# An attention kernel that splits its exponentials between two engines: three weighted pieces instead of four equal ones on VectorE

## The chip, the cores and the metric

The kernel runs on one core of one Trainium2 chip. The metric is the device time of one execution in microseconds (us). Most executions agree within 0.3%. Five engines matter: PE (TensorE, matrix multiply), DVE (VectorE), ACT (ScalarE), POOL (GpSimd) and SP (SyncE, which issues transfers). They run their own fixed lists of instructions and wait for each other by semaphores.

## The reference, cut to what matters

Two attention branches share the input x (2048 x 512, 32 heads of 16 columns). Branch A is full softmax attention, branch B a local one over 8 earlier positions with stride 2. A sigmoid gate mixes them.

```python
q, k, v = qkv[0], qkv[1], qkv[2]                      # 32 heads, 2048 positions, 16 columns
scores = jnp.einsum("bhqd,bhkd->bhqk", q, k) * scale   # 32 x 2048 x 2048 values
p = _softmax(scores, axis=-1)
o = jnp.einsum("bhqk,bhkd->bhqd", p, v)
...                                                    # branch B: 8 positions per query
return g * a + (1 - g) * b
```

Branch A asks for 32 x 2048 x 2048 exponentials. The kernel cuts them into 2048 items of 128 keys x 512 queries (128 partitions x 512 columns).

## The kernel before

ACT computes the exponential of two or three items at a time (1024 or 1536 columns), straight from the score banks, the memory into which PE writes the scores. DVE takes the other items by an arithmetic form: it writes a scaled and shifted score as a 16-bit integer, whose bits, read as a 16-bit float, are a rough exponential ("first piece"). Copies of it with another integer added are the same curve, shifted ("second-stage pieces"), made for up to four items at once. PE multiplies each piece with the values v and adds all pieces up, so that their errors partly cancel. Before, there are four pieces with equal weight:

```python
PW_S = tuple(s - math.log2(4.604879) for s in (0.0, 0.51171875, 0.1953125, -0.22070312))
NP_ = len(PW_S)
...
def exp_dve(slot_item):            # first piece: 512 columns, from a score bank
    return nc.vector.tensor_scalar(out=self.yb[bt["buf"]][:, 0, i * 512:(i + 1) * 512], in0=bank[:],
                                   scalar1=A, scalar2=1024.0 * (15.0 + PW_S[0]), op0=ALU.mult, op1=ALU.add)
def piece(bt, k):                  # second-stage piece k: up to 4 items at once
    return nc.vector.tensor_scalar(out=y[:, k, 0:n], in0=y[:, 0, 0:n],
                            scalar1=float(round(1024.0 * (PW_S[k] - PW_S[0]))), scalar2=None, op0=ALU.add)
...
nc.scalar.activation(out=self.pt[pi[0]][pi[1]][:, 0:n * 512],      # ACT: 2 or 3 items
                     in_=self.aslot[si][:, 0:n, :].rearrange("p a b -> p (a b)"), func=ACT.Exp, scale=SCALE)
...
nc.tensor.matmul(out=out, lhsT=v, rhs=r, start=start, stop=stop, tile_position=(0, 32 * j))  # weighted values
```

The order of all instructions is fixed when the program is built: the kernel's own scheduler walks through the work with its estimates of durations and decides, group by group, whether DVE takes items. "The plan of limits" is a table of 64 settings for each of eleven rules (how much work may wait for DVE, when PE turns to other work, and so on), one setting for each 32 items. A key tile is 128 keys, a key chunk four key tiles; the keys are made ready chunk by chunk, and DVE copies each result from its bank (its "evacuation"). A group of scores is held back until the keys that it may need are ready:

```python
def kq_ok(self, rem, geo, p, n, now):
    ...
        kts = sorted(kt for r in rem[b] for kt in r)[:n - left]
        ...
        for d in [self.qdone.get((ct, qc))] + [self.kdone.get((ct, kt // 4)) for kt in kts if ct or kt]:
            if d is not None and (d.end is None or d.end > now):
                return False
```

The lines of the profile name these places: L1509 (first piece), L1515 (second-stage pieces), L1580 (weighted values), L1774 (scores) and L1828 (ACT's exponentials). In the changed kernel the same five are L1533, L1539, L1605, L1801 and L1855.

Of the kernel before, what the change touches and what calls it, by code (L numbers as in the profile page):

```python
# [19 lines left out]
P = 128  # L20
S = 2048
D = 512
H = 32
# [13 lines left out]
SAFE_A = 8.5  # L37
BDEN_MIN, BDEN_MAX = 1e-30, 1e30

PW_S = tuple(s - math.log2(4.604879) for s in (0.0, 0.51171875, 0.1953125, -0.22070312))  # L40
NP_ = len(PW_S)

ACT_W = (3, 2)
NPT = (4, 4)
# [18 lines left out]
    order=((-1, 1, 0, 2, 3), (-1, 0, 2, 1, 3), (-1, 0, 1, 2, 3), (-1, 0, 1, 2, 1), (1, 0, 1, 2, 3)),  # L63
)
STRETCH = dict(
    backlog="2123224322422022220413433124322022122202222223242202222242220222",
    backlog_s="2222222312432222422021322322222202212222042122213222222022222323",
    part_us="2220421041243222243202020241242042210223124202210222222222222220",
    misc_slack="0004233313424222221242320140242224122321112121323222222242210222",
    urgent="2322222222200222222212213221131222034112012232322222222021222222",  # L70
    fit="2241222322244222322212212022422212422422222223222222222222222222",
    port="2220222202243220222020324222224422222202222222221322222222301322",
    alone="2212222122222114022222243221222222222322242231222232222233002222",
    grab="1222212222214222222222222222222224421342244213222222222422222422",
    lend="2220222222231202222224132222224232322212222244232122222242212422",
    order="2222432212022222320131412123232222203202222020223222222222222222",
)
SLOT_D = 3
D_LAST = 58
# [6 lines left out]
def _ap(t, offset, dims):  # L86
    return bass.AP(t.tensor, offset, [list(d) for d in dims])

def head_of(g, j):
    return 8 * (g // 2) + (g % 2) + 2 * j  # L90
# [654 lines left out]
class _Fast:  # L745
# [15 lines left out]
    def setup(self):  # L761
# [9 lines left out]
        self.qs = [c([P, 512], BF16, name=f"qs{i}") for i in range(2)]  # L771
        self.vaug = c([P, NKT * H * VS + 32], BF16, name="vaug")
        self.vaug4 = self.vaug[:, 0:NKT * H * VS].rearrange("p (t h e) -> p t h e", t=NKT, h=H, e=VS)
        self.pt = [[c([P, w * 512], BF16, name=f"pt{a}_{i}") for i in range(n)]
                   for a, (w, n) in enumerate(zip(ACT_W, NPT))]
        self.yb = [c([P, NP_, YB_ITEMS * 512], I16, name=f"yb{i}") for i in range(NYB)]
# [66 lines left out]
        nc.gpsimd.memset(self.vaug4[:, :, :, DH:VS], 1.0)  # L843
        nc.gpsimd.memset(self.vaug4[:, :, 8, 0:DH], 0.0)
        nc.gpsimd.memset(self.vaug[:, NKT * H * VS:NKT * H * VS + 32], 0.0)
        nc.gpsimd.memset(self.halo[:], 0.0)
        self.idx = pidx, pf, ei, ef
        nc.gpsimd.memset(self.ones[:], 1.0)
# [48 lines left out]
    def v_evac(self, st0, nst, h0, h1):  # L897
        n = (h1 - h0) * DH
        self.nc.vector.tensor_copy(out=self.vaug4[:, st0:st0 + nst, h0:h1, 0:DH],  # L899
                                   in_=self.misc[:, 0:nst * n].rearrange("p (t h e) -> p t h e", t=nst, e=DH))  # L900

    def k_evac(self, ct, sc):
        self.nc.vector.tensor_copy(out=self.kT[ct % 2][:, sc * 512:(sc + 1) * 512], in_=self.misc[:])
# [93 lines left out]
    def jobs(self):  # L997
# [58 lines left out]
                                               n=16 if (ct, sc) == (3, 3) else 8)  # L1056
        for st in range(0, NKT, 2):
            ch = self.chain([("PE", 2 * 4 * 0.06, lambda st=st: self.v_mm(st, 2, 0, 8)),
                             ("DVE", T_D1(256), lambda st=st: self.v_evac(st, 2, 0, 8))],
                            due=4 * st - 4 if st else -20, rel=max(1, 4 * st), deps=xs[st // 4])  # L1060
            vdone[(0, st)] = vdone[(0, st + 1)] = ch[-1]
        for st in range(NKT):
            ch = self.chain([("PE", 4 * 0.162, lambda st=st: self.v_mm(st, 1, 8, H)),
                             ("DVE", T_D1(384), lambda st=st: self.v_evac(st, 1, 8, H))],
                            due=512 - 100 + 4 * st, rel=80 + 20 * st)
            for ct in range(1, 4):
                vdone[(ct, st)] = ch[-1]
# [368 lines left out]
    def run(self):  # L1436
# [81 lines left out]
        def close_batch():  # L1518
            nonlocal batch
            bt = batch  # L1520
            batch = None
            n = len(bt["items"]) * 512
            bt["refs"] = NP_ * len(bt["items"])
            parts = [dict(n=NP_) for _ in bt["items"]]

            def done(k, end):
                for i, it in enumerate(bt["items"]):
                    add_pv(it, self.yb[bt["buf"]][:, k, i * 512:(i + 1) * 512].bitcast(F16), end, ("y", bt), parts[i])
            for k in range(1, NP_):
                s = Step("DVE", T_D4(n), lambda k=k: piece(bt, k), deps=list(bt["p1"]), due=bt["due"], cls=2)  # L1530
                s.on_done = lambda end, k=k: done(k, end)
                s.port = True
                self.steps.append(s)  # L1533
            last = bt["p1"][-1]

            def after(end, prev=last.on_done):
                prev(end)
                done(0, end)
            if last.end is None:  # L1539
                last.on_done = after  # L1540
            else:
                done(0, last.end)
# [9 lines left out]
        def emit_pv_one(j, now):  # L1552
            b, kt, r, ready, src, part = pvq[j].pop(pv_first(j, now))
            if b not in acc:
                acc_take(b)
            ct, qc, par = geo(b)
            g = 2 * ct + par
            first = (b, j) not in started
            started.add((b, j))
            part["n"] -= 1  # L1560
            if part["n"] == 0:
                jleft[(b, j)] -= 1
                left[b] -= 1
            last = jleft[(b, j)] == 0
            kind, ref = src
            if kind == "p":
                pt_refs[ref] -= 1
                if pt_refs[ref] == 0:
                    pt_free[ref] = now + 0.45
            else:  # L1570
                ref["refs"] -= 1
                if ref["refs"] == 0:
                    yb_free[ref["buf"]] = now + 0.45
            out = self.flex[acc[b]][32 * j:32 * j + 32, :]
            parts = [(g, r, out)] if b < NB - 2 else [(2 * ct + k, r[:, 256 * k:256 * k + 256], out[:, 256 * k:256 * k + 256])
                                                      for k in range(2)]

            def mm(g, r, out, start, stop):
                v = _ap(self.vaug, self.vaug4[:, kt, head_of(g, j), 0:1].offset, [self.vaug.ap[0], [1, 32]])
                nc.tensor.matmul(out=out, lhsT=v, rhs=r, start=start, stop=stop, tile_position=(0, 32 * j))  # L1580
            return [lambda k=k, a=a: mm(*a, first and k == 0, last and k == len(parts) - 1) for k, a in enumerate(parts)]

# [115 lines left out]

        def d_wanted(now, flex=True):

            if p >= N - 8 or p % 64 >= D_LAST:
                return False
            if batch is None and min(yb_free) > now:
                return False
            if flex and min(fx_free) > now:
                return False
            ready = [s for s in self.steps if s.rel <= p and s.eng in ("PE", "DVE") and ready_time(s) <= now + 1.5]
            if flex and any(s.acq and s.due <= p + tune("misc_slack") for s in ready):
                return False
            load = max(0.0, t["DVE"] - now) + sum(s.cost for s in ready if s.eng == "DVE")  # L1710
            return load < tune("backlog" if flex else "backlog_s")

        def draw(used, dve=False):


            nonlocal p
            b = p // 64
            js = [j for j in range(4) if rem[b][j]]
            js = [j for j in js if j not in used] or js
            if dve:  # L1720
                bj = [it[2] for it in batch["items"]] if batch is not None else []
                j = min(js, key=lambda j: (j in bj, dcount.get((b, j), 0), -len(rem[b][j]), j))
            else:
                j = min(js, key=lambda j: (-len(rem[b][j]), j))
            used.append(j)
            p += 1
            return b, rem[b][j].pop(0), j

        def d_add(it, bank, p1done):
            nonlocal batch  # L1730
# [58 lines left out]
        while True:  # L1789
# [173 lines left out]
                            wake = min(wake, est)  # L1963
            if not did:
                t[eng] = max(min(wake, max(others, now) + 0.02 if others > now else now + 0.02), now + 0.005)
        self.BP["2"].release()

    def kq_ok(self, rem, geo, p, n, now):
        left = 0
        for b in range(p // 64, NG * NQC):  # L1970
            ct, qc, par = geo(b)
            kts = sorted(kt for r in rem[b] for kt in r)[:n - left]
            left += len(kts)
            for d in [self.qdone.get((ct, qc))] + [self.kdone.get((ct, kt // 4)) for kt in kts if ct or kt]:
                if d is not None and (d.end is None or d.end > now):
                    return False
            if left >= n:
                break
        return True
# [31 lines left out]
```

## Time and profile before

The kernel before took 744.03 us (median of 3 runs, 743.74 to 744.54). Its page of the profiled execution says, in the part on busy time and the part on 40 slices of the span (each digit is the busy share of one slice in tenths):

```profile
span 741.4 us, 21444 instructions
PE 705.9 (95%) x8713; PEld 233.9 (32%) x8713; DVE 692.8 (93%) x1180; ACT 723.2 (98%) x699; POOL 204.4 (28%) x212
...
ACT  6999999999999999999999999999999999999994
```

ACT is busy except in the first and the last slice. The stretches view (busy us of each engine in a window, with the number of instructions) shows how complete this is in the middle:

```profile
80.00:120.00 40.00, 39.28 (x486) 12.23 (x483) 39.52 (x68) 39.96 (x40) 0.00 (x0) 1.00 0.10 22
400.00:440.00 40.00, 37.78 (x403) 11.65 (x399) 37.88 (x64) 40.00 (x37) 22.70 (x20) 1.00 0.46 124
```

The columns are the length, then PE, PE's weight loads, DVE, ACT and POOL, then the clock and the transfers. ACT stands at 39.96 and 40.00 of 40 us. PE and DVE are close to full too. The Trainium skill ("Perfetto Trace Analysis", Identifying the Most-Contended Engine) says that occupancy is a fair measure for ACT and DVE, and a poor one for matmuls.

ACT's timeline (start, duration of the record, instruction) gives the cost of one exponential:

```profile
299.12 1.19 ACT L1828 ACTIVATE pt_2_85<-fps 128x1024 bf16<-128x1024 f32 x1
300.03 1.20 ACT L1828 ACTIVATE pt_0_87<-fps 128x1024 bf16<-128x1024 f32 x1
300.93 1.64 ACT L1828 ACTIVATE pt_1_84<-fps 128x1536 bf16<-128x1536 f32 x1
302.26 1.23 ACT L1828 ACTIVATE pt_1_88<-fps 128x1024 bf16<-128x1024 f32 x1
```

The records overlap: they last 1.19 and 1.64 us, but the starts are 0.91 and 1.33 us apart. Only the distance of starts may be summed. With 484 exponentials of 1024 columns at 0.9065 us and 201 of 1536 at 1.333 us, ACT's list is 706.7 us long and holds 1571 of the 2048 items.

DVE's part, in the view of groups kept apart by shape (count, busy us, mean ns of one record, idle time before and its releaser), one of three buffers shown of each:

```profile
L1509 DVE TENSOR_SCALAR yb_92<-fps 128x512 int16<-128x512 f32 x162 | 106.2, 679 | 6.7 <-PE fps L1774 6.3
L1515 DVE TENSOR_SCALAR yb_92<-yb_92 128x2048 int16<-128x2048 int16 x111 | 73.0, 686 | 0.3
```

A second-stage piece of four items costs as much as a first piece of one item (both about 0.60 us start to start): it reads 16-bit data from SBUF, the first piece reads a score bank. This fits the Trainium skill ("VectorE: DVE Perf Modes", Mode 4×_2P), which gives four elements per cycle for such operands.

The head, that is the first 40 us, in which inputs are still being prepared, from ACT's timeline:

```profile
8.22 1.02 ACT L1828 ACTIVATE pt_0_83<-fps 128x1024 bf16<-128x1024 f32 x1 [0.54 <-PE fps L1774]
9.14 1.02 ACT L1828 ACTIVATE pt_0_87<-fps 128x1024 bf16<-128x1024 f32 x1
10.38 1.02 ACT L1828 ACTIVATE pt_1_84<-fps 128x1024 bf16<-128x1024 f32 x1 [0.22 <-PE fps L1774]
11.30 1.02 ACT L1828 ACTIVATE pt_1_88<-fps 128x1024 bf16<-128x1024 f32 x1
12.20 1.03 ACT L1828 ACTIVATE pt_2_85<-fps 128x1024 bf16<-128x1024 f32 x1
14.88 1.02 ACT L1828 ACTIVATE pt_2_89<-fps 128x1024 bf16<-128x1024 f32 x1 [1.65 <-PE fps L1774]
```

ACT starts at 8.22 us, does five exponentials (ten items), and then waits 1.65 us for scores.

### The profile page before, as it was taken

The numbers are of one execution on the slowest core, as the hardware profiler recorded it, in microseconds if no ns is written. First come the engines' busy times: TensorE is split into PE (matmuls) and PEld (weight loads), VectorE is DVE, ScalarE is ACT, GpSimd is POOL, SyncE is SP. The second block draws the span as 40 slices with busy tenths as digits, with TensorE's granted clock in tenths as the row PEclk, the third lists the DMA queues.
The fourth block names the chain that finished last, engine by engine and source line by source line (L and its number), as shares of the span: only waits on it lengthen the run. The fifth ranks groups of instructions, "written<-read, shape, count | busy, mean of one in ns | idle before, by whom it ended". The sixth has DMA issues, their size and how long they took to land.

```text
span 741.4 us, 21444 instructions
## 1 busy us (share of the span) xinstructions
PE 705.9 (95%) x8713; PEld 233.9 (32%) x8713; DVE 692.8 (93%) x1180; ACT 723.2 (98%) x699; POOL 204.4 (28%) x212
## 2 busy tenths in 40 slices
PE   9999999999999999998989999999999999999996
PEld 4422333333333222332222232332233232333343
DVE  6899999998999999999999999999899999899985
ACT  6999999999999999999999999999999999999994
POOL 2142000000003321322002555646544564534000
PEclk9999999999999999999999999999999999999999
DMA  5001010001000000001032546566555456422001
GB/s 165 3 18 50 8 39 1 2 2 46 2 9 9 23 1 3 8 2 38 23 118 84 147 130 160 129 137 152 140 142 128 105 125 156 120 72 58 9 23 35
DMA packets 63723, 48.59 MB, mean 66 GB/s; under 512 B 21760, under 2 KB 63232, under 8 KB 63488
## 3 DMA queue, kind: packets, MB, share of 16 engines
q1 hardware_dynamic: 62912, 45.70, 24.4%
q8 instruction: 70, 1.15, 0.7%
q0 software_dynamic: 288, 1.05, 0.4%
q10 hardware_dynamic: 416, 0.39, 0.2%
q14 instruction: 37, 0.30, 0.1%
HBM read 39.85 MB, written 5.26 MB: 61 GB/s over the span
## 4 chain that ended last, share of the span: by engine, by line
ACT 39%; PE 37%; issue 11%; DVE 10%; SPq 1%; DMA 0%; POOL 0%; ACTq 0%; DVEq 0%; POOLq 0%
PE fps L1774 13%; PE fps L1580 12%; PE fps L871 9%; ACT pt_0_83 L1828 6%; ACT pt_3_86 L1828 5%; ACT pt_2_85 L1828 5%; ACT pt_0_87 L1828 5%; ACT pt_3_90 L1828 5%; ACT pt_1_84 L1828 4%; ACT pt_2_89 L1828 4%; ACT pt_1_88 L1828 4%; DVE yb_92 L1509 2%; DVE yb_93 L1509 1%; DVE yb_91 L1509 1%; DVE yb_93 L1515 1%
## 5 line engine op out<-in xcount | busy, mean ns | idle before, releaser
L1580 PEld LDWEIGHTS <-vaug 128*32 128x32 bf16 x3697 | 86.3, 94 | 135.4 <-issue 112.2
L1828 ACT ACTIVATE pt_0_83<-fps 128x1536 bf16<-128x1536 f32 (+1 forms) x87 | 122.2, 1405 | 0.5 <-PE fps L1774 0.5
L1828 ACT ACTIVATE pt_3_86<-fps 128x1536 bf16<-128x1536 f32 (+1 forms) x85 | 117.5, 1382 | 0.0
L1828 ACT ACTIVATE pt_1_84<-fps 128x1536 bf16<-128x1536 f32 (+1 forms) x85 | 115.6, 1360 | 0.4 <-PE fps L1774 0.4
L1828 ACT ACTIVATE pt_2_85<-fps 128x1024 bf16<-128x1024 f32 (+1 forms) x86 | 115.4, 1341 | 0.1
L1509 DVE TENSOR_SCALAR yb_92<-fps 128x512 int16<-128x512 f32 x162 | 106.2, 679 | 6.7 <-PE fps L1774 6.3
L1509 DVE TENSOR_SCALAR yb_93<-fps 128x512 int16<-128x512 f32 x159 | 104.9, 680 | 5.4 <-PE fps L1774 5.1
L1509 DVE TENSOR_SCALAR yb_91<-fps 128x512 int16<-128x512 f32 x156 | 102.8, 679 | 7.7 <-PE fps L1774 7.4
L1580 PE MATMUL fps<-yb_92,vaug 128*32 128x512 f16 (+1 forms) x696 | 100.9, 368 | 0.0
L1580 PE MATMUL fps<-yb_93,vaug 128*32 128x512 f16 (+1 forms) x668 | 99.0, 373 | 0.7 <-DVE vaug L899 0.5
L1580 PE MATMUL fps<-yb_91,vaug 128*32 128x512 f16 (+1 forms) x664 | 98.8, 370 | 0.3 <-DVE yb_91 L1515 0.3
L871 PE MATMUL fps<-xT,ww 128*32 128x512 bf16 (+2 forms) x1296 | 98.1, 380 | 0.0
L1828 ACT ACTIVATE pt_2_89<-fps 128x1024 bf16<-128x1024 f32 x85 | 96.2, 1132 | 1.7 <-PE fps L1774 1.7
L1828 ACT ACTIVATE pt_0_87<-fps 128x1024 bf16<-128x1024 f32 x87 | 97.5, 1121 | 0.0
L1828 ACT ACTIVATE pt_3_90<-fps 128x1024 bf16<-128x1024 f32 x85 | 95.8, 1127 | 0.2 <-ACT pt_2_85 L1828 0.2
L1828 ACT ACTIVATE pt_1_88<-fps 128x1024 bf16<-128x1024 f32 x85 | 95.1, 1118 | 0.7 <-PE fps L1774 0.6
L1774 PEld LDWEIGHTS <-kT_73 32*128 32x128 bf16 x1024 | 47.2, 91 | 147.1 <-issue 144.1
L1774 PEld LDWEIGHTS <-kT_72 32*128 32x128 bf16 x1024 | 45.2, 91 | 145.0 <-issue 139.9
L1515 DVE TENSOR_SCALAR yb_92<-yb_92 128x2048 int16<-128x2048 int16 (+2 forms) x129 | 80.5, 655 | 0.4
L1515 DVE TENSOR_SCALAR yb_93<-yb_93 128x2048 int16<-128x2048 int16 (+3 forms) x126 | 79.5, 661 | 0.3
L1515 DVE TENSOR_SCALAR yb_91<-yb_91 128x2048 int16<-128x2048 int16 (+3 forms) x129 | 78.9, 642 | 0.2
L1177 POOL TENSOR_TENSOR prod_821<-bq_809,bk_810 128x512 bf16<-128x512 bf16 x32 | 34.0, 1076 | 114.7 <-DVE yb_93 L1515 52.6
(189 smaller groups left out, 1260.3 us busy)
## 6 DMA issues: line engine op xcount, KB each, us to landing
vw_5734<-v_dram SPq DMA_DIRECT2D x64, 128.0 KB, 3.1
vw_5735<-v_dram SPq DMA_DIRECT2D x64, 128.0 KB, 3.2
er<-er_dram SPq DMA_DIRECT2D x128, 64.0 KB, 3.1
erb_5730<-er_dram SPq DMA_DIRECT2D x64, 64.0 KB, 3.2
erb_5731<-er_dram SPq DMA_DIRECT2D x64, 64.0 KB, 3.3
out_dram<-ob SPq DMA_DIRECT2D x15, 128.0 KB, 1.8
ww<-in_B_wqkv_dram SPq DMA_DIRECT2D x12, 128.0 KB, 2.7
ww<-in_A_wqkv_dram SPq DMA_DIRECT2D x8, 128.0 KB, 3.1
```

Source lines behind the costliest of these rows:

```text
L871: self.nc.tensor.matmul(out=out_ps[32 * c:32 * c + 32, 0:n], lhsT=lhsT_of(c), rhs=rhs, start=start, stop=stop, tile_position=(0, 32 * c))
L1177: return e.tensor_tensor(out=pr[m % 2][:, a:b], in0=bq[ct][:, a:b], in1=bk[ct][:, o + a:o + b], op=ALU.mult)
L1509: return nc.vector.tensor_scalar(out=self.yb[bt["buf"]][:, 0, i * 512:(i + 1) * 512], in0=bank[:], scalar1=A, scalar2=1024.0 * (15.0 + PW_ ...
L1515: return nc.vector.tensor_scalar(out=y[:, k, 0:n], in0=y[:, 0, 0:n], scalar1=float(round(1024.0 * (PW_S[k] - PW_S[0]))), scalar2=None, op0 ...
L1580: nc.tensor.matmul(out=out, lhsT=v, rhs=r, start=start, stop=stop, tile_position=(0, 32 * j))
L1774: nc.tensor.matmul(out=dst, lhsT=self.kT[ct % 2][32 * j:32 * j + 32, kt * 128:(kt + 1) * 128], rhs=self.qm[(4 * ct + qc) % NQM][par][32 * ...
L1828: nc.scalar.activation(out=self.pt[pi[0]][pi[1]][:, 0:n * 512], in_=self.aslot[si][:, 0:n, :].rearrange("p a b -> p (a b)"), func=ACT.Exp, ...
```

## The change: its intent, and the diff

Three pieces with the weights 1, 1.265625 and 0.796875 take the place of four equal ones. This removes one second-stage instruction per batch from DVE and one weighted-value matmul per item of DVE from PE. The weights cannot sit in the pieces, so they sit in two scaled copies of v, kept for six of the sixteen key tiles only; DVE therefore takes items of these six key tiles, ACT prefers the others. DVE makes the copies, with 24 more instructions. The plan of limits was made anew.

```diff
-PW_S = tuple(s - math.log2(4.604879) for s in (0.0, 0.51171875, 0.1953125, -0.22070312))
+PW_W = (1.0, 1.265625, 0.796875)
+PW_S = tuple(s - math.log2(3.127444) for s in (0.0, -0.3330078125, 0.3330078125))
 NP_ = len(PW_S)
+KD = (2, 4, 7, 9, 12, 14)
...                                     # STRETCH: some settings of the plan changed
+    def v_scaled(self, st0, nst, h0, h1, k):
+        for st in range(st0, st0 + nst):
+            if st in KD:
+                self.nc.vector.tensor_scalar(out=self.vw4[k][:, KD.index(st), h0:h1, 0:DH], in0=...,
+                                             scalar1=PW_W[k], scalar2=None, op0=ALU.mult)
...
-                v = _ap(self.vaug, self.vaug4[:, kt, head_of(g, j), 0:1].offset, [self.vaug.ap[0], [1, 32]])
+                t_, t4, i = (self.vw[w], self.vw4[w], KD.index(kt)) if w else (self.vaug, self.vaug4, kt)
+                v = _ap(t_, t4[:, i, head_of(g, j), 0:1].offset, [t_.ap[0], [1, 32]])
...                                     # draw(): DVE's items come from KD, ACT's from the rest first
-            return b, rem[b][j].pop(0), j
+            kt = next((k for k in rem[b][j] if (k in KD) == dve), rem[b][j][0])
...                                     # kq_ok(): which keys a group of scores may need
-            kts = sorted(kt for r in rem[b] for kt in r)[:n - left]
+            kts = sorted(kt for r in rem[b] for kt in r if kt not in KD)[:n - left]
+            kts += sorted(kt for r in rem[b] for kt in r if kt in KD)[:n - len(kts) if len(kts) < n - left else 4]
```

More of the change, by code (lines that the diff above doesn't have):

```diff
@@ L38 @@
 BDEN_MIN, BDEN_MAX = 1e-30, 1e30
-PW_S = tuple(s - math.log2(4.604879) for s in (0.0, 0.51171875, 0.1953125, -0.22070312))
+PW_W = (1.0, 1.265625, 0.796875)
+PW_S = tuple(s - math.log2(3.127444) for s in (0.0, -0.3330078125, 0.3330078125))
 NP_ = len(PW_S)
+KD = (2, 4, 7, 9, 12, 14)
+NOT_KD = tuple(k for k in range(16) if k not in KD)
 ACT_W = (3, 2)
@@ L65 @@
 STRETCH = dict(
-    backlog="2123224322422022220413433124322022122202222223242202222242220222",
-    backlog_s="2222222312432222422021322322222202212222042122213222222022222323",
-    part_us="2220421041243222243202020241242042210223124202210222222222222220",
-    misc_slack="0004233313424222221242320140242224122321112121323222222242210222",
-    urgent="2322222222200222222212213221131222034112012232322222222021222222",
-    fit="2241222322244222322212212022422212422422222223222222222222222222",
-    port="2220222202243220222020324222224422222202222222221322222222301322",
-    alone="2212222122222114022222243221222222222322242231222232222233002222",
-    grab="1222212222214222222222222222222224421342244213222222222422222422",
-    lend="2220222222231202222224132222224232322212222244232122222242212422",
-    order="2222432212022222320131412123232222203202222020223222222222222222",
+    backlog="4213224322422022220413433124322022122202222223242202222212220022",
+    backlog_s="2202222312432222422021322322222202212222042122213222222022222323",
+    part_us="2220421041243222243202020241242042211223124202210222222222222220",
+    misc_slack="0004233313424222221242320140240224120321112121323222222242210222",
+    urgent="2322222222200222222212213221431222034112012232322222222021222222",
+    fit="2421222322244222322212212022422212421422222223222222222022222222",
+    port="2223222202243220222020324222224422222202222222221322222222341322",
+    alone="2211222122222114022222243221222222221322242231222232222233302222",
+    grab="1222212222214222222222222222222224411342244213222222222422422422",
+    lend="4220222222233202222224132222224232322212222244232122222242311422",
+    order="2222432212022222320131412123232222203202222120223222222222222222",
 )
@@ L773, in setup @@
         self.vaug4 = self.vaug[:, 0:NKT * H * VS].rearrange("p (t h e) -> p t h e", t=NKT, h=H, e=VS)
+        nk = len(KD) * H * VS
+        self.vw = [None] + [c([P, nk + 32], BF16, name=f"vaugw{i}") for i in range(1, NP_)]
+        self.vw4 = [None] + [w[:, 0:nk].rearrange("p (t h e) -> p t h e", t=len(KD), h=H, e=VS) for w in self.vw[1:]]
         self.pt = [[c([P, w * 512], BF16, name=f"pt{a}_{i}") for i in range(n)]
@@ L845, in setup @@
         nc.gpsimd.memset(self.vaug[:, NKT * H * VS:NKT * H * VS + 32], 0.0)
+        for w, v, v4 in zip(PW_W[1:], self.vw[1:], self.vw4[1:]):
+            nc.gpsimd.memset(v4[:, :, :, DH:VS], w)
+            nc.gpsimd.memset(v4[:, :, 8, 0:DH], 0.0)
+            nc.gpsimd.memset(v[:, len(KD) * H * VS:], 0.0)
         nc.gpsimd.memset(self.halo[:], 0.0)
@@ L900, in v_evac @@
                                    in_=self.misc[:, 0:nst * n].rearrange("p (t h e) -> p t h e", t=nst, e=DH))
+    def v_scaled(self, st0, nst, h0, h1, k):
+        n = (h1 - h0) * DH
+        for st in range(st0, st0 + nst):
+            if st in KD:
+                o = (st - st0) * n
+                self.nc.vector.tensor_scalar(out=self.vw4[k][:, KD.index(st), h0:h1, 0:DH],
+                                             in0=self.misc[:, o:o + n].rearrange("p (h e) -> p h e", e=DH),
+                                             scalar1=PW_W[k], scalar2=None, op0=ALU.mult)
     def k_evac(self, ct, sc):
@@ L1058, in jobs @@
             ch = self.chain([("PE", 2 * 4 * 0.06, lambda st=st: self.v_mm(st, 2, 0, 8)),
-                             ("DVE", T_D1(256), lambda st=st: self.v_evac(st, 2, 0, 8))],
+                             ("DVE", T_D1(256), lambda st=st: self.v_evac(st, 2, 0, 8))] + [
+                                 ("DVE", T_D1(128), lambda st=st, k=k: self.v_scaled(st, 2, 0, 8, k))
+                                 for k in range(1, NP_) for t in (st, st + 1) if t in KD],
                             due=4 * st - 4 if st else -20, rel=max(1, 4 * st), deps=xs[st // 4])
@@ L1063, in jobs @@
             ch = self.chain([("PE", 4 * 0.162, lambda st=st: self.v_mm(st, 1, 8, H)),
-                             ("DVE", T_D1(384), lambda st=st: self.v_evac(st, 1, 8, H))],
+                             ("DVE", T_D1(384), lambda st=st: self.v_evac(st, 1, 8, H))] + [
+                                 ("DVE", T_D1(384), lambda st=st, k=k: self.v_scaled(st, 1, 8, H, k))
+                                 for k in range(1, NP_) if st in KD],
                             due=512 - 100 + 4 * st, rel=80 + 20 * st)
@@ L1527, in done @@
                 for i, it in enumerate(bt["items"]):
-                    add_pv(it, self.yb[bt["buf"]][:, k, i * 512:(i + 1) * 512].bitcast(F16), end, ("y", bt), parts[i])
+                    add_pv(it, self.yb[bt["buf"]][:, k, i * 512:(i + 1) * 512].bitcast(F16), end, ("y", bt, k), parts[i])
             for k in range(1, NP_):
@@ L1564, in emit_pv_one @@
             last = jleft[(b, j)] == 0
-            kind, ref = src
+            kind, ref, w = (*src, 0)[:3]
             if kind == "p":
@@ L1699, in d_wanted @@
         def d_wanted(now, flex=True):
-            if p >= N - 8 or p % 64 >= D_LAST:
+            if p >= N - 8 or p % 64 >= D_LAST or not any(k in KD for r in rem[p // 64] for k in r):
                 return False
@@ L1717, in draw @@
             b = p // 64
-            js = [j for j in range(4) if rem[b][j]]
+            js = [j for j in range(4) if (any(k in KD for k in rem[b][j]) if dve else rem[b][j])]
             js = [j for j in js if j not in used] or js
@@ L1726, in draw @@
             p += 1
-            return b, rem[b][j].pop(0), j
+            kt = next((k for k in rem[b][j] if (k in KD) == dve), rem[b][j][0])
+            rem[b][j].remove(kt)
+            return b, kt, j
         def d_add(it, bank, p1done):
@@ L1965, in run @@
                 t[eng] = max(min(wake, max(others, now) + 0.02 if others > now else now + 0.02), now + 0.005)
+        self.t_end = dict(t)
         self.BP["2"].release()
@@ L1971, in kq_ok @@
             ct, qc, par = geo(b)
-            kts = sorted(kt for r in rem[b] for kt in r)[:n - left]
-            left += len(kts)
+            kts = sorted(kt for r in rem[b] for kt in r if kt not in KD)[:n - left]
+            kts += sorted(kt for r in rem[b] for kt in r if kt in KD)[:n - len(kts) if len(kts) < n - left else 4]
+            left += min(n - left, sum(map(len, rem[b])))
             for d in [self.qdone.get((ct, qc))] + [self.kdone.get((ct, kt // 4)) for kt in kts if ct or kt]:
```

## The prediction

> **What bounds the kernel now.** The page's busy table gives ACT 723.2 of 741.4 us (98%), PE 95%, DVE 93%. In the stretch-by-stretch table of busy time ACT is at 39.6 to 40.0 of every 40 us from 40 to 720. The timeline of ACT shows its exponentials start to start: 0.91 us for 1024 columns (two items), 1.33 us for 1536 (three items). Their records are longer (1.12 and 1.56 us) because neighbours overlap. There are 484 of the first and 201 of the second: 1571 of 2048 score items, about 440 + 267 = 707 us. Around that stand about 8.2 us before the first exponential, some 10 us after the last one starts, some 5 us of other ACT work and small gaps. The time is therefore head + ACT's exponentials + tail. PE and DVE matter only where they make ACT wait; the waits of ACT on PE sum to a few us, mostly in the first 40 us. The Trainium skill ("ScalarE: Activation LUTs", What ACT_TABLE_LOAD costs) puts a function at 0.833 ns per element whatever it computes; the step 0.91 to 1.33 us for 512 more columns agrees (0.82).
>
> **What the change does, counted from the built instruction order of both kernels.**
> - ACT: 1536-column exponentials 201 -> 193, 1024-column ones 484 -> 484. Items on ACT 1571 -> 1547. That is 8 x 1.33 = 10.7 us less.
> - DVE: first pieces 477 -> 501 (+24 at 0.60 us start to start = +14.5 us). Second-stage pieces of 2048 columns 324 -> 226, all sizes 384 -> 270 (about 0.61 us for a large one: -65 us). Twelve 128-column and twelve 384-column scaled copies of v are added (estimate from the 256-column evacuation at 0.33 and the 384-column one at 0.47 us: about +8 us). Net about -42 us: DVE falls from 693 to about 650 us.
> - PE: weighted-value matmuls per DVE item 4 -> 3, so 3479 -> 3050; four share about 0.22 us, so about -23 us, less a few more filler matmuls (124 -> 157). PE loses load too.
>
> **On the critical path.** The relief of DVE and PE is mostly off the path: about 42 and 23 us disappear, but the plan hands only 24 more items to DVE. Only these 24 items, 10.7 us, shorten the saturated engine. The rest becomes idle time of DVE (about 88% busy) and PE. ACT should stay about 98% busy. The head may lose or gain about 1 us: scaled copies compete with the evacuations of x, k and v. The tail is unchanged.
>
> **Predicted time: 733.3 us, 8 in 10 between 729.5 and 737.5 (ratio about 0.986).** Chances: faster by over 2% (below 729.2) 0.09, within 2% 0.90, slower 0.01.
>
> **What would show it right.** ACT busy falls to 711 to 714 us and remains about 98% of the span, saturated in every middle stretch; start-to-start times unchanged; DVE about 645 to 655 us busy; second-stage pieces still 0.61 us; tail about as long as before.
>
> **What would make it wrong.** If ACT shows new gaps behind the score matmuls (DVE items now come from only six key tiles, hence come in bursts and hold score banks longer; or the first key tiles of the second quarter are wanted earlier), the gain shrinks and ACT's busy share falls. If the new plan also removes the gaps of ACT left now (about 13 us over the middle, read as start-to-start time above the usual), the gain exceeds 10.7 us and could pass 2%.

## The result, and the profile after

The changed kernel took 736.29 us (median of 4 runs, 735.97 to 737.3), the kernel before beside it 744.21 us. The ratio is 0.9899, 95% interval 0.9885 to 0.9913. (The ratios here and below are not quite the ratios of the medians, which would be 0.9894 here.) The time fell by 7.9 us, the 10.7 us of the prediction less about 3.

The page after, and two stretches:

```profile
span 734.5 us, 20496 instructions
PE 690.6 (94%) x8285; PEld 229.1 (31%) x8285; DVE 653.6 (89%) x1114; ACT 713.5 (97%) x691; POOL 204.6 (28%) x218
...
ACT  4999999999999999999999999999999999999994
...
80.00:120.00 40.00, 38.80 (x446) 12.03 (x445) 35.04 (x61) 40.00 (x41) 0.00 (x0) 1.00 0.04 9
400.00:440.00 40.00, 37.33 (x379) 11.79 (x376) 36.58 (x62) 40.00 (x39) 12.44 (x11) 1.00 0.47 127
```

ACT is still full in the middle. DVE's busy time fell by 39 us, PE's by 15 us, ACT's by 9.7 us. The first slice of ACT fell from 6 tenths to 4: the head is worse.

The groups by shape show what moved (buffers stand under one name here):

```profile
L1855 ACT ACTIVATE pt<-fps 128x1024 bf16<-128x1024 f32 x484 | 489.2, 1118 | 4.9 <-PE fps L1801 3.9 <-PE fps L1605 0.4
L1855 ACT ACTIVATE pt<-fps 128x1536 bf16<-128x1536 f32 x193 | 300.6, 1558 | 1.7 <-PE fps L1801 1.5
L1533 DVE TENSOR_SCALAR yb<-fps 128x512 int16<-128x512 f32 x501 | 325.6, 681 | 31.7 <-PE fps L1801 30.3
L1539 DVE TENSOR_SCALAR yb<-yb 128x2048 int16<-128x2048 int16 x226 | 151.5, 695 | 0.5
L918 DVE TENSOR_SCALAR vaugw<-fps 128x384 bf16<-128x384 f32 x12 | 6.4, 550 | 0.0
```

ACT has 193 instead of 201 wide exponentials, the rest is equal: 1547 items, 696.0 us. The two widths have kept their durations.

The head, from ACT's timeline (its second line merges 19 exponentials without a gap between them) and PE's:

```profile
9.19 1.45 ACT L1855 ACTIVATE pt<-fps 128x1536 bf16<-128x1536 f32 x1 [1.27 <-PE fps L1801]
14.58 19.90 ACT L1855 ACTIVATE pt<-fps 128x1024 bf16<-128x1024 f32 x19 [3.94 <-PE fps L1801]
```

```profile
8.71 0.39 PE L1801 MATMUL fps<-qm,kT 32*128 32x512 bf16 x4 [0.67 <-DVE kT L974]
9.04 0.63 PE L881 MATMUL fps<-wAv,xT 128*32 128x128 bf16 x32
9.60 2.01 PE L983 MATMUL fps<-ident,x_in 128*128 128x128 bf16 x32
11.60 1.05 PE L881 MATMUL fps<-xT,ww 128*32 128x512 bf16 x16
12.58 0.62 PE L983 MATMUL fps<-ident,x_in 128*128 128x128 bf16 x8
13.13 1.05 PE L881 MATMUL fps<-xT,ww 128*32 128x512 bf16 x16
14.11 0.61 PE L1801 MATMUL fps<-qm,kT 32*128 32x512 bf16 x7
```

The first group of scores waits for the second part of the keys (L974), because it holds an item of key tile 2 for DVE. Then five steps of preparation (values, transposes of x, two projections of keys) stand in PE's list before the second group of scores at 14.11 us. ACT does three items before 14.6 us; the kernel before had done ten by 14.9.

A ledger of ACT makes the sum exact. It is worked out from the starts of ACT's instructions in the trace: "gaps" are the distances of starts beyond the usual 0.9065 us (1024 columns), 1.333 us (1536) and 0.48 us (512), from the first exponential on. "Ends" is the end of the last exponential, "tail" what follows it. Nine other ACT instructions of 512 columns (4.3 us) and the overhang of the last record are nearly the same in all rows and not listed, which is why the terms add up to some 4.5 us less than the ends.

| us | first exponential | ACT's list | gaps to 40 us | gaps after | last one ends | tail | span |
|---|---|---|---|---|---|---|---|
| before | 8.22 | 706.7 | 2.98 | 9.08 | 731.49 | 9.9 | 741.4 |
| after | 9.19 | 696.0 | 4.45 | 10.52 | 724.61 | 9.9 | 734.5 |
| difference | +0.97 | -10.7 | +1.47 | +1.44 | -6.88 | 0 | -6.9 |

(The last exponential is 1024 columns wide after and 1536 before; that accounts for the 0.1 us that the first four terms leave of the ends.) So the gain expected from ACT's list came in full. Of the 3.9 us that were lost again, 2.4 us lie in the head and 1.4 us in small gaps spread over the rest. Not all of the 0.97 us belongs to the change: PE's first projection (L871, L881 after) started at 5.81 us before and at 6.12 us after, and in a second profile of the changed kernel (a_again below) at 5.72 us. From there to the first exponential it is 2.40 us before and 3.06 us after. So about 0.7 us is due to the change; the other 0.3 us lie before that projection, where two profiles of the same kernel differ by 0.4 us.

### The profile page after: what moved, and what is told of

It reads as the page before. It is cut to its first block, busy times and chain, and to the rows that moved or that the text cites. A ratio compares the mean times of both kernels' runs of the same rounds, so it can differ in the third digit from the quotient of the medians.

```text
span 734.5 us, 20496 instructions
## 1 busy us (share of the span) xinstructions
PE 690.6 (94%) x8285; PEld 229.1 (31%) x8285; DVE 653.6 (89%) x1114; ACT 713.5 (97%) x691; POOL 204.6 (28%) x218
## 3 DMA queue, kind: packets, MB, share of 16 engines
q1 hardware_dynamic: 62912, 45.70, 24.3%
## 4 chain that ended last, share of the span: by engine, by line
ACT 43%; PE 29%; issue 14%; DVE 12%; DMA 1%; SPq 1%; POOL 0%; ACTq 0%; POOLq 0%
ACT pt L1855 42%; PE fps L1801 10%; PE fps L1605 8%; PE fps L881 7%; DVE yb L1533 6%; DVE yb L1539 3%; PE fps L1350 1%; DMA vw<-v_dram 1%; DVE t L1628 1%; PE fps L1215 1%; ACT er L1220 1%; PE fps L954 0%; DVE oT L1641 0%; DVE t L1637 0%; PE fps L983 0%
## 5 line engine op out<-in xcount | busy, mean ns | idle before, releaser
L1855 ACT ACTIVATE pt<-fps 128x1024 bf16<-128x1024 f32 (+1 forms) x677 | 708.0, 1243 | 6.6 <-PE fps L1801 5.4
L1533 DVE TENSOR_SCALAR yb<-fps 128x512 int16<-128x512 f32 x501 | 325.6, 681 | 31.7 <-PE fps L1801 30.3
L1801 PE MATMUL fps<-qm,kT 32*128 32x512 bf16 x2048 | 309.9, 382 | 32.8 <-ACT pt L1855 24.3
L1605 PE MATMUL fps<-pt,vaug 128*32 128x512 bf16 (+1 forms) x1646 | 237.2, 373 | 0.7 <-DVE bq L1177 0.5
L1801 PEld LDWEIGHTS <-kT 32*128 32x128 bf16 x2048 | 94.8, 91 | 296.7 <-issue 290.1
L1539 DVE TENSOR_SCALAR yb<-yb 128x2048 int16<-128x2048 int16 (+3 forms) x270 | 168.6, 655 | 0.8
L1605 PE MATMUL fps<-yb,vaugw 128*32 128x512 f16 (+1 forms) x1060 | 160.2, 372 | 0.5 <-DVE yb L1539 0.5
L1332 POOL TENSOR_TENSOR er<-er,vw 128x512 bf16<-128x512 bf16 x64 | 72.7, 1154 | 136.2 <-DMA erb<-er_dram 70.8
L881 PE MATMUL fps<-xT,ww 128*32 128x512 bf16 (+2 forms) x1296 | 97.4, 381 | 0.2
L1605 PE MATMUL fps<-yb,vaug 128*32 128x512 f16 (+1 forms) x530 | 92.5, 372 | 0.0
L1332 POOL TENSOR_TENSOR erb<-erb,vw 128x512 bf16<-128x512 bf16 x64 | 72.4, 1155 | 60.6 <-DVE yb L1539 24.9
L881 PEld LDWEIGHTS <-ww 128*32 128x32 bf16 x1296 | 23.9, 95 | 33.8 <-issue 28.4
L881 PE MATMUL fps<-woB,oB 128*32 128x512 bf16 x256 | 19.6, 383 | 0.3 <-DVE yb L1533 0.2
L881 PE MATMUL fps<-wAv,oT 128*32 128x512 bf16 x256 | 19.6, 384 | 0.1
```

Source lines behind the costliest of these rows:

```text
L881: self.nc.tensor.matmul(out=out_ps[32 * c:32 * c + 32, 0:n], lhsT=lhsT_of(c), rhs=rhs, start=start, stop=stop, tile_position=(0, 32 * c))
L1332: return nc.gpsimd.tensor_tensor(out=st_["erb"][m % 4][:, g, :], in0=st_["erb"][m % 4][:, g, :], in1=st_["vw"][m % 2][:, g, :], op=ALU.mult)
L1801: nc.tensor.matmul(out=dst, lhsT=self.kT[ct % 2][32 * j:32 * j + 32, kt * 128:(kt + 1) * 128], rhs=self.qm[(4 * ct + qc) % NQM][par][32 * ...
```

## The experiments

The theory: the time is ACT's list plus head, gaps and tail. The relief of DVE and PE shortens nothing by itself; it pays for the items that DVE takes over. The rivals: the relief itself makes the kernel faster; or one of pieces and plan alone does it; or the scaled copies cause the loss in the head. One more rival was not run: that a fresh search of the plan would have helped the old four-piece code as well. Each run has the kernel before beside it; the medians of the kernel before were 743.2 to 744.0 us.

### b_no4: the fourth piece left out, everything else as before

```diff
         def piece(bt, k):
+            if k == 3:
+                return None
...
             def mm(g, r, out, start, stop):
+                if gone and not (start or stop):      # gone: a matmul of piece 3
+                    return
```

> The kernel before, in its own unchanged order, with the fourth piece left out: 128 second-stage instructions of DVE and 435 weighted-value matmuls of PE are not issued; the result is wrong on purpose. ACT's list is untouched (201 + 484 exponentials). Theory (only ACT's list of exponentials sets the time; relief of DVE and PE is off the path): 744 us, within 2 us of the kernel before; DVE busy about 693 - 75 = 618 us, PE's matmul work about 23 us less. Rival (the relief of DVE or PE is what makes the changed kernel faster, directly): 5 us or more faster than before.

Measured: 742.43 us against 743.21, ratio 0.9989 (0.9972 to 1.0005). The result stayed within the tolerance of the check of outputs. The page:

```profile
span 740.1 us, 20434 instructions
PE 698.3 (94%) x8278; PEld 230.5 (31%) x8278; DVE 629.5 (85%) x1052; ACT 722.9 (98%) x699; POOL 204.0 (28%) x212
```

DVE's busy time fell by 63 us (75 expected), more than in the real change. PE lost 435 matmuls but only 8 us of busy time (23 expected): four matmuls start every 0.22 us while a record lasts about 0.37 us, so the records overlap and busy time does not show the load that went. ACT was busy for 722.9 us, as before, and the time moved by 0.8 us, within the noise (the interval holds 1). The relief itself is worth nothing that could be measured, as the theory has it. The rival expected 5 us or more.

### a_dve_load: DVE's relief taken back, PE's kept

```diff
             y = self.yb[bt["buf"]]
+            if k == 1:                                # the same piece, computed twice
+                nc.vector.tensor_scalar(out=y[:, k, 0:n], in0=y[:, 0, 0:n],
+                                        scalar1=float(round(1024.0 * (PW_S[k] - PW_S[0]))), scalar2=None, op0=ALU.add)
             return nc.vector.tensor_scalar(out=y[:, k, 0:n], in0=y[:, 0, 0:n],
```

> The changed kernel in its own order, but each batch's first shifted piece is computed twice by DVE, to the same place: 135 more second-stage instructions, so DVE has about what a four-piece form would give it (654 + about 78 = about 730 us) while PE and ACT's list are unchanged; result right. Theory (the removed piece matters because without that relief DVE could not carry 501 items): DVE then has no slack, ACT gets gaps behind the score matmuls, time rises to 742-760 us. Rival (DVE had room for 24 more items anyway, the new plan alone did it): under 738 us.

Measured: 805.73 us, ratio 1.0833 (1.0811 to 1.0856). The direction is the theory's, the size is not: 69 us more than the changed kernel, where at most 24 were expected. Page and waits of ACT and PE (who waited for whom: us in total, times, longest):

```profile
span 804.7 us, 20624 instructions
PE 719.9 (89%) x8285; PEld 231.2 (29%) x8285; DVE 738.5 (92%) x1249; ACT 731.5 (91%) x691; POOL 205.4 (26%) x218
...
ACT pt L1858 <- PE fps L1804: 51.2, 106, 3.9
...
PE fps L1608 <- DVE yb L1542: 26.1, 62, 1.0
PE fps L1804 <- DVE yb L1533: 18.8, 57, 1.5
```

(The edit shifts the later lines by 3.) DVE is busy for 738.5 us, 85 us more. That alone is more than the changed kernel's whole span of 734.5 us, so with this load on DVE, at these durations, no order could have kept that time. But not all of DVE's idle time was used either: it fell only from 81 to 66 us. The order was fixed for a shorter DVE, and PE's waits for DVE's pieces and first pieces rose from 4.3 us (0.5 + 3.8 in the changed kernel) to 44.9 us. ACT waits behind PE: its gaps after 40 us are 78.4 us in the ledger, against 10.5. The expectation counted DVE's busy time only (about 730 us), and not these waits. The granted PE clock also fell to 0.7 in three of the 40 slices (0.976 in the mean); what that added was not tested.

### a_pe_load: PE's relief taken back, DVE's kept

```diff
                 nc.tensor.matmul(out=out, lhsT=v, rhs=r, start=start, stop=stop, tile_position=(0, 32 * j))
+                if w == 1 and not (start or stop):    # zero weights: adds nothing
+                    nc.tensor.matmul(out=out, lhsT=self.wz[:, 0:32], rhs=r, start=False, stop=False,
+                                     tile_position=(0, 32 * j))
```

> The changed kernel in its own order, with one more matmul of zero weights behind each weighted-value matmul of the second piece (530 more, about 530/4 x 0.22 = 29 us of PE), so PE has about the matmuls of a four-piece form while DVE and ACT's list are unchanged; result right. Theory (both reliefs are needed; PE serves ACT between two score groups and has little slack): slower, 740-755 us. Rival (only the relief of DVE pays for the 24 items): within 2 us of 736.

Measured: 752.62 us, ratio 1.0123 (1.0106 to 1.014), 16 us more than the changed kernel. ACT's gaps after 40 us rose from 10.5 to 26.1 us in the ledger; the list is that of the changed kernel, and head and tail differ from it by less than 0.4 us each. PE's waits for ACT show where its slack went, first the changed kernel, then this one:

```profile
PE fps L1801 <- ACT pt L1855: 24.3, 84, 0.8
```

```profile
PE fps L1804 <- ACT pt L1858: 11.3, 40, 0.7
```

PE no longer stands ready for 24 us when ACT frees a score bank, but for 11. So both reliefs were needed for this order: neither engine could take its old load back. It also corrects what a busy share of 94% seems to say. PE's share is the same in b_no4, whose order holds room for 435 more matmuls (with them it is the kernel before, at the same time), and in the changed kernel, which lost 16 us when PE was given some 29 us of matmuls (an estimate: 530 / 4 x 0.22 us). This agrees with what the Trainium skill ("Perfetto Trace Analysis", Identifying the Most-Contended Engine) says of matmul busy time.

These two runs load an order that was made for less. They do not show what the best order for the heavier load would cost; the kernel before is such an order, at 744 us.

### a_oldplan and b_newplan: the pieces without the plan, the plan without the pieces

```diff
-STRETCH = dict(...the new plan...)      # a_oldplan: the changed kernel
+STRETCH = dict(...the old plan...)
```

```diff
-STRETCH = dict(...the old plan...)      # b_newplan: the kernel before
+STRETCH = dict(...the new plan...)
```

> Three pieces with the plan of limits of the kernel before (plan undone, pieces kept). Built order: 203 + 475 exponentials on ACT and one of 512 columns, 701.7 us at the start-to-start times of the trace, against 696.0 in the changed kernel and 706.7 before. Theory (time = ACT's list + head + gaps + tail): at least 736.3 + 5.7 = 742 us, more if an untuned plan leaves gaps on ACT: 742-754. Rival (the new pieces alone bring the gain, the plan is cosmetic): 734-738 us.

> The kernel before (four equal pieces) with the new plan of limits: the plan alone, without the pieces. Built order: 225 + 460 exponentials on ACT and one of 512 columns, 717.4 us at the start-to-start times of the trace (706.7 in the kernel before); only 452 items go to DVE. Theory (the plan fits only the code it was made for; time = ACT's list + head + gaps + tail): at least 743.2 + 10.7 = 754 us, to 768 with new gaps. Rival (the plan is what brings the gain): under 740 us.

Measured: a_oldplan 754.3 us, ratio 1.0141 (1.0124 to 1.0158), 0.3 us above the range expected; b_newplan 765.83 us, ratio 1.03 (1.0284 to 1.0316). Each half alone makes the kernel slower, by 11 and by 22 us. The ledger says where, beside the two kernels:

| us | first exponential | ACT's list | gaps to 40 us | gaps after | last one ends | span |
|---|---|---|---|---|---|---|
| before | 8.22 | 706.7 | 2.98 | 9.08 | 731.49 | 741.4 |
| b_newplan | 8.81 | 717.4 | 3.84 | 18.64 | 753.22 | 762.9 |
| a_oldplan | 9.05 | 701.7 | 6.40 | 20.67 | 742.28 | 753.0 |
| after | 9.19 | 696.0 | 4.45 | 10.52 | 724.61 | 734.5 |

A plan that was not made for the code puts fewer items on DVE (452 in b_newplan and 488 in a_oldplan, against 477 before and 501 after) and leaves about 20 us of gaps on ACT instead of 10. With three pieces and the old plan the list is 5 us shorter than before, and the kernel still loses. A part of these gaps lies where the granted PE clock fell, which it does in no slice of the two kernels. The stretches view of a_oldplan (the last three columns are the clock, DMA share and GB/s):

```profile
301.00:321.00 20.00, 17.45 (x157) 4.66 (x155) 15.21 (x22) 18.25 (x19) 5.28 (x6) 0.74 0.00 1
```

The clock is 0.74 here and ACT has 18.25 of 20 us. In these two orders the scheduler also placed fewer filler matmuls, which keep PE at work (93 in a_oldplan and 64 in b_newplan, against 124 before and 157 after). Whether that let the clock fall was not tested.

The head of a_oldplan has the same first gap of 4.06 us as the changed kernel, although its plan is the old one; b_newplan, with the new plan, has 1.77 us at the place where the kernel before has 1.78. This gap therefore belongs to the code of the change, not to the plan.

The two runs show that pieces and plan belong together. They do not show what the search for a plan is worth by itself: the four-piece code was never given a plan newly searched for it.

### a_ksplit: the cut in the first evacuation of the keys

```diff
-        for a, b, bank in ((0, 128, self.flex[3]), (128, 512, self.flex[0])):
+        for a, b, bank in ((0, 384, self.flex[3]), (384, 512, self.flex[0])):
```

> The changed kernel in its own order; only the cut of the first evacuation of the keys moves from column 128 to column 384, so that key tile 2, which DVE's first item now uses, comes with the first part. The first group of scores then waits for one evacuation instead of two. Theory (in the changed kernel the head lost about 0.7 us to this): first exponential at about 8.5 us instead of 9.2, whole time 0.4 to 0.8 us shorter, about 735.7. Rival (the head is bound by the later key chunk that the second group of scores waits for): first exponential earlier, but the gap after it longer by as much and the time unchanged.

Measured: 736.61 us (735.71 to 738.56, five runs), ratio 0.9913 (0.9897 to 0.9929), no faster than the changed kernel. ACT's timeline:

```profile
9.00 1.45 ACT L1855 ACTIVATE pt<-fps 128x1536 bf16<-128x1536 f32 x1 [1.05 <-PE fps L1801]
14.48 1.02 ACT L1855 ACTIVATE pt<-fps 128x1024 bf16<-128x1024 f32 x1 [4.03 <-PE fps L1801]
```

The first exponential came at 9.00 us, not at 8.5, and the second group as late as ever. The changed kernel itself started at 9.19 us in one profile and at 8.78 us in another (a_again below), so the start alone says nothing. Counted from PE's first projection it says more: 2.84 us here, 3.06 to 3.15 us in the six profiles that have the changed kernel's order of the first groups and the old cut, 2.29 to 2.40 us in the three profiles of four-piece code and in a_head. So the cut won back 0.2 to 0.3 us of about 0.7, and the time did not follow. The second group is what counts, and it comes after a fixed row of preparations in PE's list.

### a_no_scaled: without the scaled copies of v

```diff
-        for st in range(st0, st0 + nst):
+        for st in range(0):                            # no copy is made
...
-                t_, t4, i = (self.vw[w], self.vw4[w], KD.index(kt)) if w else (self.vaug, self.vaug4, kt)
+                t_, t4, i = self.vaug, self.vaug4, kt  # all weights 1
```

> The changed kernel in its own order without the 24 scaled copies of v: the three pieces all take plain v (weights 1, wrong on purpose). DVE loses about 9 us, 12 of the 24 in the head. Theory (the copies sit in slack of DVE, off the path): within 1 us of the changed kernel, DVE about 645 us busy, first gap of ACT unchanged at about 4 us. Rival (the copies delay the evacuations of the head and cause the head's loss): 2 us or more shorter, the gap after the first exponential gone.

Measured: 736.28 us, ratio 0.9901 (0.9886 to 0.9916), the same as the changed kernel to 0.1 us; outputs within the tolerance again. DVE was busy for 646.5 us instead of 653.6, the gap after the first exponential stayed at 4.06 us. The copies cost 7 us of DVE in its slack and no time. The rival for the head's loss falls.

### a_head and a_again: the head's order mended, and the changed kernel once more

```diff
-            if p >= N - 8 or p % 64 >= D_LAST or not any(k in KD for r in rem[p // 64] for k in r):
+            if p == 0 or p >= N - 8 or p % 64 >= D_LAST or not any(k in KD for r in rem[p // 64] for k in r):
...
-            kts += sorted(kt for r in rem[b] for kt in r if kt in KD)[:n - len(kts) if len(kts) < n - left else 4]
+            kts += sorted(kt for r in rem[b] for kt in r if kt in KD)[:n - len(kts) if len(kts) < n - left else 2]
...                                     # STRETCH: another plan, searched for this code
```

> The changed kernel with the head's order mended: the check that holds back a group of scores looks two items of DVE ahead in the list of DVE's key tiles instead of four (four reached key tile 4, which needs the second key chunk, at the second group already), and the very first group holds no item for DVE. Because any edit changes the order of the whole program, the plan of limits was searched anew for this code. Built order: 189 + 489 exponentials, 1545 items on ACT (1547 in the changed kernel), 695.2 us at the start-to-start times. Theory (the changed kernel lost about 3 us in the head to this order): first exponential near 8.2 us, no gap of 4 us after it; 736.3 - 0.8 - 3 = 732.5 us, if the gaps of ACT behind 40 us stay at about 10 us; 731 to 734.5. Rival (what is lost in the head is no loss, it comes back as other gaps): 735.5 us or more.

> The changed kernel once more, unaltered, on the same chip as the one above, for a direct comparison: 736.3 us, within 1 us; ratio to the kernel before about 0.990.

Measured on one chip: a_head 734.43 us, ratio 0.9877 (0.986 to 0.9893); a_again 736.31 us, ratio 0.9903 (0.9886 to 0.9919); the kernel before 743.44 us. a_head changes three things at once (the look-ahead, the first group and the plan), so its gain can't be put down to one of them. a_head beats both kernels, by 9.0 and 1.9 us. The gain over the changed kernel is half of the expected 3.8 us. PE's list in the head of a_head:

```profile
9.63 0.40 PE L1801 MATMUL fps<-qm,kT 32*128 32x512 bf16 x4
9.96 0.62 PE L983 MATMUL fps<-ident,x_in 128*128 128x128 bf16 x8
10.51 0.39 PE L1801 MATMUL fps<-qm,kT 32*128 32x512 bf16 x3
...
14.14 0.60 PE L1801 MATMUL fps<-qm,kT 32*128 32x512 bf16 x6
```

Groups of scores now stand at 9.63 and 10.51 us between the preparations, and the first exponential came at 7.91 us. But the group at 14.14 us did not move, and the ledger finds two gaps where one was:

| us | first exponential | ACT's list | gaps to 40 us | gaps after | last one ends | span |
|---|---|---|---|---|---|---|
| a_again | 8.78 | 696.0 | 4.45 | 10.61 | 724.30 | 734.2 |
| a_head | 7.91 | 695.2 | 4.81 | 10.72 | 723.11 | 732.8 |

The gap of 4.06 us became one of 2.22 us (before 14.6 us) and a new one of 2.41 us (before 25.8 us). This second one ends with the scores that follow the evacuation of another key chunk (24.72 us). So the gain in the profiles is the earlier start, 0.9 us (0.1 us of it before PE's first projection), and a list 0.8 us shorter, less 0.5 us of longer gaps. The time lies in the theory's range, but both the theory and its rival are half right: the earlier start was won back, but about as much as the gap of 4 us lost came back as another wait in the head. What would remove that wait is open; it would need keys prepared earlier, and no run here tried it.

## Why the prediction was right

The measured 736.3 us lies in the predicted range, 1.2 us below its upper end, and 3 us above the single number 733.3. The mechanism held; one term of the sum, the head, was too small.

**Bound by ACT: right.** ACT was full in every middle stretch before and after, and b_no4 shows that taking 63 us from DVE and 435 matmuls from PE leaves the time where it was, within the noise.

**ACT's list 10.7 us shorter: right.** 193 + 484 exponentials ran at the same distances of starts; ACT's busy time fell to 713.5 us (711 to 714 predicted), its share to 97%.

**DVE down to about 650 us, PE lower: right for DVE, for PE in direction.** DVE 653.6 us (645 to 655 predicted). PE's busy time fell by 15 us, where about 23 us, less a few fillers, had been counted. The scaled copies were put at 8 us and are worth 7 us, by a_no_scaled.

**"The relief of DVE and PE is mostly off the path": right, with an addition.** As a direct gain it is worth nothing (b_no4). But a_dve_load and a_pe_load show that this order needs both: 69 and 16 us are lost when either is taken back. The relief is what the 24 items were bought with.

**"The head may lose or gain about 1 us": this term was mis-sized.** The head lost 2.4 us to 40 us: the first exponential 0.97 us later (about 0.7 us of it from the change), the gaps 1.47 us longer. The prediction looked at the scaled copies, which cost nothing there. What ACT waited for is the order of scores: the first group waits for key tile 2, and the second one stands behind the preparation of the second key chunk. The first puts the start about 0.7 us later; what the second costs is not settled, since a_head, which changed it, has two gaps of 2.2 and 2.4 us in its place. The prediction did name "the first key tiles of the second quarter are wanted earlier" among what could make it wrong.

**Gaps of ACT after 40 us: 1.4 us longer**, 10.5 instead of 9.1, in small pieces, none over 0.6 us. The prediction gave no number for them. No run isolates their cause.

Together, 10.7 - 2.4 - 1.4 = 6.9 us, the difference of the two profiled spans; the medians differ by 7.9 us, as single executions vary by about 1 us.

What stays open is what the search for a plan is worth without the pieces, and why the new plan gives DVE 24 items and no more, although DVE is idle for 80 us. DVE's wait for scores rose from 19 to 30 us, which points to score banks or PE's service rather than to DVE's speed, but no run took that apart.

## What to carry to other kernels

When one engine is full from head to tail, count how many of its instructions a change removes and multiply by the distance of their starts; relief on other engines counts only as far as it lets them take work from the full one. With a fixed order of instructions, a change and its schedule are one thing: here each half alone cost 11 or 22 us, together they gained 8. Look at the head apart from the middle, and at which data the first groups of work need: here the changed kernel had three items to start on before the second key chunk was ready, where the kernel before had ten, and the full engine stood for 4 us.

## What the Trainium skill lacked or had wrong

- "ScalarE: Activation LUTs" (What ACT_TABLE_LOAD costs) gives 186 ns + 0.833 ns per column for an ACTIVATE with immediate operands and an overlap of about 93 ns back to back, which makes 93 ns of fixed cost for each (an estimate from these two figures). Here starts are 0.9065 us apart at 1024 columns and 1.333 us at 1536: 0.833 ns per column holds, the fixed cost is 53 ns. The records at 1024 columns last 1.02 to 1.32 us, 1.12 in the mean, where the formula gives 1.04, and overlap by 0.1 to 0.4 us.
- "Perfetto Trace Analysis" (Identifying the Most-Contended Engine) rightly warns of matmul busy time and names MFU (the share of peak arithmetic, not worked out here) and the busy share of weight loads in its place. The share of weight loads did not tell PE's real room here: it is 31% in b_no4, which had room, and 31% in the changed kernel, which lost 16 us for about 29 us more work (a_pe_load). PE's waits for ACT did not tell it either (27.6 us in b_no4, 24.3 in the changed kernel); only the run that added load did.
- No page was found to say how little of an engine's idle time a fixed order can use: DVE was idle for 81 us of the changed kernel's 734.5; 85 us more work left it idle for 66 us, and cost 69 us.
